# One gather job per block, later blank fills and a later planned landing in a self-scheduled attention and router kernel

## The chip, the cores and the metric

The kernel runs on one core of a Trainium2 chip. The metric is the device time of one execution in microseconds (us). The core has a matrix engine (PE, with its weight loads as PEld), a vector engine (DVE), a scalar engine (ACT), a general engine (POOL) and a queue engine (SP) that mostly starts transfers. Each engine runs its instructions in the order in which the program lists them; the engines wait for each other by semaphores.

## The reference, cut to what matters

```
def phi(x):                                   # 8 x 8 products of two small projections
    a = einsum('rd,bhsd->bhsr', S1, x); b = einsum('rd,bhsd->bhsr', S2, x)
    return einsum('bhsi,bhsj->bhsij', a, b).reshape(..., 64)
q_p, k_p = phi(q), phi(k)                     # q, k, v: 4 batches, 4 heads, 1088 tokens, 32 wide
kv  = einsum('bhsf,bhsd->bhfd', k_p, v);  z = k_p.sum(axis=2)
x   = (q_p @ kv) / (q_p @ z + 1e-6)           # 4352 tokens x 128
noisy = x @ w_gate + log1p(exp(x @ w_noise)) * noise
top2, weights = two best of 8 experts per token, softmax of the two
out[t] = sum over the two experts e of t: weight * (relu(x[t] @ w1[e]) @ w2[e])   # 128 -> 1024 -> 128
```

## The kernel before, in words

**Waves and blocks.** The tokens are routed in five waves: the first half of batch 0 (wave 0, 512 tokens), the rest of batch 0 (wave 1), and batches 1, 2 and 3 (waves 2, 3 and 4). `router` picks the two experts of each token of a wave and their rows, and POOL scatters the scaled tokens (`xg`) by indirect DMAs into the DRAM table `xs`, which has a stretch of rows for every expert ("xs<-xg,to"). Rows that no token may fill are zeroed beforehand by seven blank fills, `clear(0)` to `clear(6)` ("xs<-pad"). A scatter waits for the fills of the rows that its wave can reach: wave 2 for fills 0 to 3, wave 3 for 0 to 4, wave 4 for all.

`block(u, ...)` is one expert's share of a wave: 128 tokens for u below 16, 256 later, 128 again in the last wave of blocks. Its tokens are fetched from `xs` into `xb`, turned into `bT`, multiplied with w1 (`hp`, line 1117), passed through ReLU on ACT (`h`, line 1125), multiplied with w2 (`acc`, line 1132), copied to `y` and scattered by POOL to the DRAM table `pairs`. Blocks 0 to 3 don't go through DRAM: one-hot squares (`o` or `h` tiles) gather their tokens straight from `x` by four matmuls each (line 1074). Blocks 4 to 7 are fetched by POOL's own queue and turned on PE (line 1096). From block 8 on SP fetches (four DMAs a block) and DVE turns (line 1106). The row numbers of a wave come by a small fetch `ix`.

**The attention.** Per batch: DVE turns k and q (`kT`, `qT`, lines 577 and 579), PE projects them (`feat`, line 595), DVE turns the result (`ab`, line 603) and multiplies out `phk` and `phq` (line 618), PE sums `kv` (line 665) and folds the gate weights in (line 686), then turns `phq` (line 713, copied by ACT to `pT`) and multiplies it with the folded table (line 724, copied by ACT to `nd`). From `nd` DVE makes the gates of the router.

**What sets the order.** Nothing is scheduled by hand. Each piece of work is a `Job` with engines, an estimated cost, a landing time (`lat`), a priority and its data. `Plan.order` runs a small model: at each step it takes, of the jobs that could start soonest, the one with the lowest priority number, and so writes one list for every engine. SP transfers take part in a model of the DMA rate, and `lanes` limits how many transfers are planned in flight. PSUM tiles come from pools of two buffers each (`bank`, `feat`, `hp`, `acc`); `bank` serves the gather, the turned blocks, lines 713 and 724 and the counts. Only the order comes from the model; on the chip the waits come from the data. The transfers marked `held`, late inputs and late fills, also wait on the chip for POOL's four fetches.

Of the kernel before, what the change touches and what calls it, by code (L numbers as in the profile page):

```python
# [36 lines left out]
class Plan:  # L37
# [50 lines left out]
    def order(self):  # L88
# [18 lines left out]
        while cand:  # L107
# [37 lines left out]
            if j.size is not None:  # L145
                moved = max(moved, j.end + 0.6) + j.size / self.RATE
                j.done = max(j.done, moved + 0.8 if e == "SP" else j.end + 1.4 + 2 * j.size / self.RATE)
                if e != "POOL":
                    lanes.append(j.done)
            j.opens = [b for b in j.opens if not b.placed]  # L150
            for b in j.opens:
                b.placed = True
# [23 lines left out]
def kernel(  # L176
# [27 lines left out]
    C = 8  # L204
# [30 lines left out]
    def add(engines, cost, emit, **kw):  # L235

        if hold and engines in ("DVE", "PE"):
            kw["after"] = tuple(kw.get("after", ())) + tuple(hold)
        elif hold and engines == EV:
            engines = "ACT"  # L240
        return plan.add(engines, cost, emit, **kw)
# [70 lines left out]
    def mm(n):  # L312
        return max(0.205, 0.016 + 0.00162 * n)
# [477 lines left out]

    BLANK = [(80, 128), (216, 256), (472, 512), (728, 768), (984, 1024), (1024, 1088), (1088, STATIC)]

    def clear(i, prio):
        lo, hi = BLANK[i]

        def done(ins):
            for w in range(NW):
                if REACH[w] <= lo:
                    apart(ins, "scatter%d" % w)  # L800
            wrote(ins, "clear%d" % i)
        g = 16 if (hi - lo) % 16 == 0 else 8
        n = (hi - lo) // g
        dma("SP", lambda: xs_e[:, lo:hi, :].rearrange("e (p c) x -> p e (c x)", c=n),
            lambda: pad[0:g, 0:n * XW].unsqueeze(1).to_broadcast([g, E, n * XW]), ["pad"], [("clear", i)], prio,
            size=4.2e3 * (hi - lo), issue=0.8, done=done, held=i > 2)

    def blanks(w):
        return [i for i, (lo, hi) in enumerate(BLANK) if lo < REACH[w]]
# [11 lines left out]
    def router(b, t0, n, w, x, den, lg, prio):  # L821
# [161 lines left out]
        for t in range(n):  # L983
            rows = slice(0, HB if t0 + t == C else P)
            xg = new("xg")
            pool_job(0.19, prio + 0.8, lambda t=t, xg=xg: G.tensor_copy(
                xg.t[:, :, D:XW].bitcast(I32), pid[:, :, b, t0 + t:t0 + t + 1]), [(xg, 9)], ["pid"])
            if den is None:
                dve(vec(2 * D), lambda t=t, xg=xg: V.tensor_tensor(
                    out=xg.t[:, :, 0:D], in0=x.t[:, t:t + 1, :].to_broadcast([P, 2, D]),  # L990
                    in1=B_["g"].t[:, :, t:t + 1].to_broadcast([P, 2, D]), op=ALU.mult), [x, "g"], [(xg, 0), (xg, 1)], late, [indexed])
            for i in range(2):
                if den is not None:
                    pool_job(gtt(D), prio + 0.9, lambda t=t, i=i, xg=xg: G.tensor_tensor(  # L994
                        out=xg.t[:, i, 0:D].rearrange("p (h d) -> p h d", h=H), in0=x.t[:, t, :, 0:DH],
                        in1=dg.t[:, i, t, :].unsqueeze(2).to_broadcast([P, H, DH]), op=ALU.mult), [(xg, i)], [x, dg], sent[-2:-1])

                def emit(e, t=t, i=i, rows=rows, xg=xg):
                    ins = pool_scatter(den is None, out=xs[:], in_=xg.t[rows, i, :], in_offset=None,
                                       out_offset=bass.IndirectOffsetOnAxis(ap=to.t[rows, i, t:t + 1], axis=0))  # L1000
                    apart(ins, "scatter", "fetch", *("clear%d" % i for i in range(len(BLANK)) if i not in blanks(w)))
                    behind(ins, *("clear%d" % i for i in blanks(w)))
                    wrote(ins, "scatter", "scatter%d" % w)
                sent.append(add("POOL", 1.67 if den is None else 1.2, emit, r=[to, (xg, i), (xg, 9)] + [("clear", i) for i in blanks(w)],
                    w=[("rows", (w, t, i))], prio=prio + 1, lat=LAND + (0.7 if w == 0 else 0.0)))
                routed.setdefault(w, []).append(("rows", (w, t, i)))
        return picked

# [35 lines left out]
    def block(u, w, e, r, n):  # L1044
# [5 lines left out]
        if u < DIRECT:  # L1050
# [7 lines left out]
            def part(c):  # L1058
                return oh.t[:, c, :] if u < DIRECT - 1 else oh.t[:, P * c:P * c + P]
# [10 lines left out]
                    r=["place", onehot["pos"], onehot["gm"]] + ([less] if u == DIRECT - 1 else []), w=[(oh, c)],  # L1070
                    prio=-900 if u == 0 else 12 + u)

            for c in range(4):
                add("PE", mm(P), lambda _, c=c: T.matmul(
                    turn.t[:, 0:P], lhsT=onehot["x"].t[:, c, :], rhs=part(c), start=(c == 0), stop=(c == 3)),
                    lat=0.15, r=[(oh, c), (onehot["x"], c - c % 2)], w=[turn], prio=p0 - 88)
        else:
            xb = new("xb")

# [208 lines left out]
    load_kq(1, "q", 45)  # L1288
    for e in range(2, E):
        load_w(e, 46 + e)  # L1290
    for i in range(2, len(BLANK)):
        clear(i, 60 if i == 2 else 290 + 2 * i)
    x, den, lg, last = queries(0, 0, 4, 10, True)
    picked = router(0, 0, 4, 0, x, den, lg, 12)
    pair_numbers(0, 0, 1, "POOL", 15)
# [6 lines left out]
    for b in range(1, B):  # L1302
        if b > 1:
            load_kq(b, "k", 80 + 100 * b)
            load_kq(b, "q", 81 + 100 * b)
            load_v(b, 82 + 100 * b)
            keys_values(b, 100 * b)
        x, den, lg, last = queries(b, 0, C + 1, 100 * b + 10)
        router(b, 0, C + 1, b + 1, x, den, lg, 100 * b + 20)
        hold.clear()  # L1310
    look(500)
    u = 0
# [64 lines left out]
```

## Time and profile before

| | us |
|---|---|
| median of three runs (lowest, highest) | 351.43 (350.46, 353.52) |
| the profiled execution | 351.54 |
| its span, first to last instruction | 349.8 |
| PE busy in the span | 325.2 |
| POOL busy | 245.4 |
| ACT busy | 137.3 |
| DVE busy | 130.9 |

Busy times of different engines overlap. The profiled execution is 1.7 us longer than its span and within 0.1 us of the median. The mean granted PE clock over the span is 0.975 of full speed.

### The profile page before, as it was taken

The numbers are of one execution on the slowest core, as the hardware profiler recorded it, in microseconds if no ns is written. First come the engines' busy times: TensorE is split into PE (matmuls) and PEld (weight loads), VectorE is DVE, ScalarE is ACT, GpSimd is POOL, SyncE is SP. The second block draws the span as 40 slices with busy tenths as digits, with TensorE's granted clock in tenths as the row PEclk, the third lists the DMA queues.
The fourth block names the chain that finished last, engine by engine and source line by source line (L and its number), as shares of the span: only waits on it lengthen the run. The fifth ranks groups of instructions, "written<-read, shape, count | busy, mean of one in ns | idle before, by whom it ended". The sixth has DMA issues, their size and how long they took to land.

```text
span 349.8 us, 8036 instructions
## 1 busy us (share of the span) xinstructions
PE 325.2 (93%) x2897; PEld 296.0 (85%) x2897; DVE 130.9 (37%) x503; ACT 137.3 (39%) x295; POOL 245.4 (70%) x466
## 2 busy tenths in 40 slices
PE   6889999996999999999999999999999999999940
PEld 2558799795979998999998999999999999999930
DVE  5889698695698719510001110012002000002001
ACT  1336445542544553333432444333433343334310
POOL 7847836968899888888898989979953345354430
PEclk9999999997899999999999999999999999999985
DMA  7999949863311155325223232255334111117103
GB/s 192 272 250 347 359 113 222 140 182 56 71 36 40 39 67 89 75 33 91 59 57 54 55 69 61 53 161 142 66 108 142 31 28 30 32 41 240 51 20 93
DMA packets 66795, 37.31 MB, mean 107 GB/s; under 512 B 48879, under 2 KB 59793, under 8 KB 66752
## 3 DMA queue, kind: packets, MB, share of 16 engines
q1 hardware_dynamic: 61344, 26.87, 33.5%
q0 software_dynamic: 4768, 9.23, 8.2%
q10 hardware_dynamic: 640, 0.67, 0.7%
q8 instruction: 23, 0.38, 0.5%
q14 instruction: 20, 0.16, 0.2%
HBM read 24.17 MB, written 12.83 MB: 106 GB/s over the span
## 4 chain that ended last, share of the span: by engine, by line
PE 40%; issue 20%; POOL 17%; DVE 11%; DMA 6%; ACT 3%; SPq 1%; POOLq 0%; DVEq 0%; ACTq 0%
PE hp L1117 17%; PE acc L1132 17%; POOL pairs L815 9%; POOL pause L816 5%; POOL xs L815 3%; DVE phq L618 2%; DMA kq<-in_q_dram 2%; DMA xs<-xg,to 2%; PE bank L724 2%; ACT h L1125 1%; PE feat L595 1%; PE bank L713 1%; POOL xg L994 1%; DMA pr<-pairs 1%; SPq L332 1%
## 5 line engine op out<-in xcount | busy, mean ns | idle before, releaser
L1132 PEld LDWEIGHTS acc<-w2s,h 128*128 128x128 f32 x1152 | 146.2, 192 | 8.3 <-ACT h L1125 2.4
L1132 PE MATMUL acc<-w2s,h 128*128 128x128 f32 x1152 | 151.0, 276 | 1.6 <-ACT h L1125 1.4
L1117 PE MATMUL hp<-bT,w1s 128*128 128x128 f32 (+1 forms) x768 | 150.1, 332 | 0.0
L1125 ACT ACTIVATE h<-hp 128x512 f32<-128x512 f32 x144 | 85.7, 597 | 125.1 <-PE hp L1117 104.5
L1117 PEld LDWEIGHTS hp<-bT,w1s 128*128 128x128 f32 x768 | 113.8, 195 | 5.8 <-ACT bT L322 0.4
L815 POOL DMA_INDIRECT pairs<-y,mine x72 | 73.4, 1020 | 57.1 <-ACT y L322 45.2
L815 POOL DMA_INDIRECT xs<-xg,to x72 | 74.3, 1032 | 21.1 <-POOL xg L994 8.1
L1106 DVE STREAM_TRANSPOSE bT<-xb 128x256 f32<-128x256 f32 (+1 forms) x40 | 15.6, 389 | 140.7 <-PE hp L1117 104.8
L816 POOL MEMSET pause<- 1x512 bf16 (+1 forms) x144 | 46.8, 325 | 0.1
L994 POOL TENSOR_TENSOR xg<-nd,dg 128x128 f32<-128x128 f32 x64 | 28.4, 445 | 3.3 <-DVE dg L961 3.3
L322 ACT COPY y<-acc 128x128 f32<-128x128 f32 (+1 forms) x48 | 15.3, 318 | 21.7 <-PE acc L1132 14.8
L1164 DVE TENSOR_TENSOR o<-pr 128x512 f32<-128x512 f32 (+2 forms) x12 | 6.8, 567 | 43.3 <-DMA pr<-pairs 41.2
L724 PEld LDWEIGHTS bank<-kvw,pT 128*128 128x128 f32 x128 | 15.2, 192 | 1.7 <-issue 1.4
L724 PE MATMUL bank<-kvw,pT 128*128 128x98 f32 x128 | 16.4, 276 | 0.2 <-ACT pT L322 0.2
L713 PE MATMUL bank<-ident,phq 128*128 128x128 f32 x72 | 12.0, 288 | 3.1 <-DVE phq L618 2.5
L322 ACT COPY pT<-bank 128x512 f32<-128x512 f32 (+1 forms) x20 | 10.8, 544 | 5.8 <-PE bank L713 4.0
L1339 PE MATMUL hp<-zb 128*128 128x512 bf16 x42 | 11.7, 426 | 1.4 <-POOL zb L434 1.4
L618 DVE TENSOR_TENSOR phk<-ab 128x512 f32<-128x512 f32 (+1 forms) x20 | 12.8, 694 | 0.0
L713 PEld LDWEIGHTS bank<-ident,phq 128*128 128x128 f32 x72 | 8.2, 147 | 5.3 <-ACT vaug L637 2.5
L618 DVE TENSOR_TENSOR phq<-ab 128x512 f32<-128x512 f32 (+1 forms) x20 | 12.5, 659 | 0.1
L322 ACT COPY nd<-bank 128x392 f32<-128x392 f32 (+1 forms) x18 | 7.9, 449 | 8.9 <-PE bank L724 6.5
L603 DVE STREAM_TRANSPOSE ab<-feat 64x32 f32<-64x32 f32 (+2 forms) x32 | 7.6, 283 | 9.0 <-PE feat L595 6.0
(166 smaller groups left out, 196.2 us busy)
## 6 DMA issues: line engine op xcount, KB each, us to landing
w1s<-in_moe_w_dram SPq DMA_DIRECT2D x8, 512.0 KB
w2s<-in_moe_w_dram SPq DMA_DIRECT2D x8, 512.0 KB
xb<-xs SPq DMA_DIRECT2D x96, 32.0 KB
pr<-pairs SPq DMA_DIRECT2D x6, 512.0 KB
kq<-in_k_dram SPq DMA_DIRECT2D x4, 544.0 KB
kq<-in_q_dram SPq DMA_DIRECT2D x4, 544.0 KB
vld<-in_v_dram SPq DMA_DIRECT2D x14, 128.0 KB
out_dram<-o SPq DMA_DIRECT2D x6, 256.0 KB
```

The lines of the kernel that those rows point to most:

```text
L322: A.copy(o, i) if e == "ACT" else V.tensor_copy(o, i)
L618: (V if e == "DVE" else G).tensor_tensor(out=dst.t[rows, c0 + i:c0 + m, :, :].rearrange("p c h (i j) -> p (c h) i j", i=R), in0=f[:, :, 0, ...
L713: T.transpose(ps.t[:, c0:c0 + P], pq.t[:, t + i, 2 * a:2 * a + 2, :].rearrange("p h f -> p (h f)"), ident[:])
L724: T.matmul(ps2.t[:, c0:c0 + 2 * YW], lhsT=pT.t[:, P * (2 * i + a):P * (2 * i + a) + P], rhs=kvw.t[:, a, :], start=True, stop=True)
L815: ins = G.indirect_dma_start(**kw)
L816: G.memset(pause[:, 0:PAUSE if fill else 2], 0.0)
L994: pool_job(gtt(D), prio + 0.9, lambda t=t, i=i, xg=xg: G.tensor_tensor(out=xg.t[:, i, 0:D].rearrange("p (h d) -> p h d", h=H), in0=x.t[:, ...
L1106: add("DVE", vec(P * n), lambda _: V.transpose(bT.t[:, 0:P * n], flat()), r=[xb], w=[bT], prio=TOP + u)
L1117: T.matmul(hp.t[:, P * n * i:P * n * (i + 1)], lhsT=w1s[:, e, P * (js * g + i):P * (js * g + i + 1)], rhs=bT.t[:, 0:P * n], start=True, st ...
L1125: A.activation(out=h.t[:], in_=hp.t[:], func=AF.Relu)
L1132: T.matmul(acc.t[:, D * c:D * c + D], lhsT=h.t[:, P * (n * i + c):P * (n * i + c + 1)], rhs=w2s[:, e, j, :], start=(j == 0 and c == 0), st ...
L1339: T.matmul(began[0][:], lhsT=zb[:, 0:P], rhs=zb[:], start=True, stop=True)
```

## The change: what it does

Three edits of the planner's input. The four gathering matmuls of block 0 stay four jobs, since the first squares come one by one; those of blocks 1 to 3 become one job of four matmuls each. Blank fills 4, 5 and 6 get a later priority and may be planned only after the mask of wave 1's router, and a late fill's planned issue time grows from 0.8 to 1.7 us. The planned landing of wave 1's scatters grows by 1.5 us, and `lanes` now counts a transfer by its own issue and the DMA rate, without the job's landing time. No instruction is added or removed; the planner writes another order.

```diff
-                    lanes.append(j.done)
+                    lanes.append(max(j.end + 2.3, moved + 0.8 if e == "SP" else 0.0))
...
-    def clear(i, prio):
+    def clear(i, prio, after=()):
...
-            size=4.2e3 * (hi - lo), issue=0.8, done=done, held=i > 2)
+            size=4.2e3 * (hi - lo), issue=1.7 if i > 2 else 0.8, done=done, held=i > 2, after=after)
...
-                    w=[("rows", (w, t, i))], prio=prio + 1, lat=LAND + (0.7 if w == 0 else 0.0)))
+                    w=[("rows", (w, t, i))], prio=prio + 1, lat=LAND + (0.7, 1.5, 0.0, 0.0, 0.0)[w]))
...
-            for c in range(4):
-                add("PE", mm(P), lambda _, c=c: T.matmul(
-                    turn.t[:, 0:P], lhsT=onehot["x"].t[:, c, :], rhs=part(c), start=(c == 0), stop=(c == 3)),
-                    lat=0.15, r=[(oh, c), (onehot["x"], c - c % 2)], w=[turn], prio=p0 - 88)
+            def gathered(_, cs):
+                for c in cs:
+                    T.matmul(turn.t[:, 0:P], lhsT=onehot["x"].t[:, c, :], rhs=part(c), start=(c == 0), stop=(c == 3))
+            for cs in ((0,), (1,), (2,), (3,)) if u == 0 else (range(4),):
+                add("PE", mm(P) * len(cs), lambda _, cs=cs: gathered(_, cs), lat=0.15,
+                    r=[(oh, c) for c in cs] + [(onehot["x"], c - c % 2) for c in cs], w=[turn], prio=p0 - 88)
...
-    for i in range(2, len(BLANK)):
-        clear(i, 60 if i == 2 else 290 + 2 * i)
+    clear(2, 60)
+    clear(3, 296)
...
-        router(b, 0, C + 1, b + 1, x, den, lg, 100 * b + 20)
+        picked = router(b, 0, C + 1, b + 1, x, den, lg, 100 * b + 20)
+        if b == 1:
+            for i in range(4, len(BLANK)):
+                clear(i, 390 + 2 * i, (picked,))
```

On PE, after block 0's second product, block 2's gather came in two halves, and block 3's as one matmul and, behind batch 1's k projection, three. Now block 1's and block 3's come whole and at once, block 1's `hp` and eight matmuls of line 713 follow, and then block 2's gather, whole too. Three places show what else has moved.

On DVE, from the turned k projection of batch 1 (`ab`) on, before: all of `phk` and the q projection come first, then wave 1's gates (`den`).

```order
L603 STREAM_TRANSPOSE ab<-feat 128x8x32
L603 STREAM_TRANSPOSE ab<-feat 64x32
L618 TENSOR_TENSOR phk<-ab 128x512 x4
L618 TENSOR_TENSOR phk<-ab 64x256
...
L618 TENSOR_TENSOR phq<-ab 128x512
L735 TENSOR_SCALAR den<-nd 128x20
```

After, wave 1's router is worked in between; its row numbers (`to`) now come before most of `phk` and all of `phq`.

```order
L603 STREAM_TRANSPOSE ab<-feat 128x8x32
L603 STREAM_TRANSPOSE ab<-feat 64x32
L735 TENSOR_SCALAR den<-nd 128x20
...
L618 TENSOR_TENSOR phk<-ab 128x512
L870 TENSOR_SCALAR up<-u 128x40
...
L618 TENSOR_TENSOR phk<-ab 128x512 x2
L922 TENSOR_SCALAR g<-g 128x5
...
L955 CAST to<-at 128x2x5
```

The factors `dg` stood ahead of `to` before and stand behind it now.

On SP, from batch 2's inputs to wave 1's fetches, before:

```order
L332 DMA vld<-in_v_dram 32x4x32 x2
L332 DMA xs<-pad 8x8x645 x2
L332 DMA xs<-pad 16x8x516 x2
L332 DMA kq<-in_k_dram 128x1088
L332 DMA kq<-in_q_dram 128x1088
...
L332 DMA ix<-xs 128x8x1
L332 DMA xb<-xs 32x4x32 x32
L332 DMA ix<-xs 128x8x1 x2
```

After:

```order
L332 DMA vld<-in_v_dram 32x4x32 x2
L332 DMA xs<-pad 8x8x645
L332 DMA kq<-in_k_dram 128x1088
L332 DMA kq<-in_q_dram 128x1088
...
L332 DMA xb<-xs 32x4x32 x32
L332 DMA xs<-pad 8x8x645
L332 DMA xs<-pad 16x8x516 x2
L332 DMA ix<-xs 128x8x1 x2
```

Fills 4, 5 and 6 have moved from between the inputs of batches 2 and 3 to behind wave 1's 32 fetches, ahead of wave 2's.

On PE, at the first block of wave 1 (block 8): before, everything of block 7, batch 2's sum (665) and the wave's counts (913, 916) stood ahead of the queries (713).

```order
L1132 MATMUL acc<-w2s,h 128x128 x8
L665 MATMUL bank<-phk,vaug 33x64 x36
L913 LDWEIGHTS earlier
...
L713 MATMUL bank<-ident,phq 128x128 x4
L686 MATMUL feat<-wg_71,kvT 64x49 x4
L1117 MATMUL hp<-bT,w1s 128x128 x12
```

After:

```order
L1134 MATMUL acc<-w2s,h 128x128 x8
L665 MATMUL bank<-phk,vaug 33x64 x36
L1119 MATMUL hp<-bT,w1s 128x128 x12
L1134 MATMUL acc<-w2s,h 128x128 x8
L686 MATMUL feat<-wg_71,kvT 64x49 x4
L1119 MATMUL hp<-bT,w1s 128x128 x4
```

Of the twelve `hp` matmuls the last four are block 8's, which need its `bT`; block 7's second product and the counts stand behind them.

## Rows read from the trace of the kernel before

**Rows 1.** Windows of 1 us, PE alone: length, busy (instructions), clock, DMA share, GB/s.

```profile
80.00:81.00 1.00, 0.86 (x23) 1.00 0.76 62
81.00:82.00 1.00, 0.19 (x2) 1.00 0.30 61
82.00:83.00 1.00, 0.00 (x0) 1.00 0.43 99
83.00:84.00 1.00, 0.02 (x1) 0.62 0.27 39
84.00:85.00 1.00, 1.00 (x4) 0.50 0.24 36
```

**Rows 2.** Timeline of PE there: start, us, operation, [idle before <- releaser].

```profile
78.19 2.33 PE L665 MATMUL bank<-phk,vaug 128*33 128x64 f32 x72
83.98 1.09 PE L713 MATMUL bank<-ident,phq 128*128 128x128 f32 x4 [2.46 <-DVE phq L618]
```

**Rows 3.** Timeline of DVE at the wait.

```profile
82.86 0.31 DVE L1106 STREAM_TRANSPOSE bT<-xb 128x128 f32<-128x128 f32 x1 [3.68 <-DMA xb<-xs]
```

**Rows 4.** The chain that ended last, wave 1's last scatter: start, us, what.

```profile
72.59 5.81 DMA xs<-xg,to
```

**Rows 5.** Timeline of SP: how long it took to issue fills, inputs, fetches.

```profile
55.73 6.80 SPq L332 DMA_DIRECT2D xs<-pad  x4
68.51 3.41 SPq L332 DMA_DIRECT2D vld<-in_v_dram  x6
78.63 0.39 SPq L332 DMA_DIRECT2D ix<-xs  x1
79.07 16.84 SPq L332 DMA_DIRECT2D xb<-xs  x32
124.14 1.12 SPq L332 DMA_DIRECT2D ix<-xs  x2
```

**Rows 6.** Windows of 2 us: PE, PEld, DVE, ACT, POOL, clock, DMA share, GB/s.

```profile
64.00:66.00 2.00, 1.85 (x39) 1.02 (x37) 1.92 (x7) 0.82 (x3) 1.80 (x4) 1.00 0.87 114
70.00:72.00 2.00, 2.00 (x20) 2.00 (x19) 1.93 (x5) 0.66 (x3) 1.83 (x4) 1.00 1.03 366
```

**Rows 7.** Timeline of DVE at wave 1's router.

```profile
45.51 0.18 DVE L735 TENSOR_SCALAR den<-nd 128x20 f32<-128x20 f32 x1 [0.19 <-ACT nd L322]
53.48 1.50 DVE L618 TENSOR_TENSOR phq<-ab 128x512 f32<-128x512 f32 x2
56.13 0.17 DVE L955 CAST to<-at 128x10 uint32<-128x10 f32 x1
```

**Rows 8.** The chain that ended last: pieces of PE's work, each matmul as two.

```profile
97.35 1.10 PE feat L595 x24
...
99.97 0.92 PE acc L1132 x8
```

**Rows 9.** Timeline of POOL: scaling and scatters of waves 1 and 2.

```profile
53.72 1.52 POOL L994 TENSOR_TENSOR xg<-nd,dg 128x128 f32<-128x128 f32 x2 [3.31 <-DVE dg L961]
57.10 1.32 POOL L815 DMA_INDIRECT xs<-xg,to  x1 [1.86 <-issue]
120.68 0.95 POOL L815 DMA_INDIRECT xs<-xg,to  x1 [0.21 <-issue]
```

**Rows 10.** Timeline of ACT: one copy of line 713's result to `pT`.

```profile
49.32 0.58 ACT L322 COPY pT<-bank 128x512 f32<-128x512 f32 x1
```

**Rows 11.** Windows of 1 and 5 us, PE alone, with the old order's small waits.

```profile
96.00:97.00 1.00, 0.86 (x9) 1.00 0.40 33
...
110.00:115.00 5.00, 4.78 (x48) 1.00 0.12 40
...
120.00:125.00 5.00, 4.67 (x41) 1.00 0.13 30
```

**Rows 12.** Timeline: wave 2's first turned block on DVE, its first use on PE.

```profile
129.56 0.45 DVE L1106 STREAM_TRANSPOSE bT<-xb 128x256 f32<-128x256 f32 x1 [8.71 <-DMA xb<-xs]
134.75 1.03 PE L1117 MATMUL hp<-bT,w1s 128*128 128x256 f32 x4
```

## The prediction

> **What bounds the kernel now.** The first view is the page's busy table: PE works 325.2 of 349.8 us, so only what makes PE stand still, or run slowly, can be won. Its slices over the span show three soft places: the start, a hole a little past 80 us, and the tail after PE's last product. The change touches neither end, so the hole is the one to read. In windows of 1 us [rows 1] PE is busy 0.86, 0.19, 0.00 and 0.02 us between 80 and 84: 1.07 of 4, so **2.93 us idle**. While it stood, the granted clock fell to 0.50, that is from 2.4 to 1.2 GHz, and it stayed there until 90 (five more windows like the last one shown). Six us of work at half speed are three us of work at full speed, so the clock cost **3.0 us** more. Together the hole costs 5.9 us, 1.7% of the run. What clock comes back to PE is worth as much as what idle time does.
>
> Why does PE stand? It waits for DVE's `phq` [rows 2], but DVE was not busy: it had sat 3.68 us in front of a `bT` that waits for wave 1's first fetched block, and `phq` stands behind that in DVE's order [rows 3]. The fetch was late because wave 1's last scatter, issued at 72.59, landed 5.81 us later [rows 4]; SP started `ix` at 78.63 [rows 5], and the first `bT` began at 82.86, 4.23 us after. So the chain is: wave 1's router on DVE, ten scatters on POOL, landing, fetch, DVE, PE.
>
> **The change, part by part.** The profiled execution took 351.54 us, within 0.1 of the median, so sums are made against it. No instruction comes or goes; the gathers, the fills and the scatters cost what they cost. What counts is the order.
>
> *Router earlier.* On PE, one group of `acc` matmuls, two groups of `hp` and batch 1's q projection now come behind the last of batch 0's queries instead of ahead of it: 0.9 + 2 x 0.9 + 1.1 = 3.8 us, a group of `hp` taken as one of `acc` [rows 8]. Against it stands a new wait, below, of 0.5. So batch 0's `nd` is complete, and DVE starts wave 1's gates, 3.3 us earlier: at 42.2 instead of 45.51 [rows 7], since DVE now does little in front of it. From there to the end of `to` DVE took 45.51 to 56.30, 10.8 us, with four pieces of `phq` in between; now three pieces of `phk` of the same shape (0.75 each by the `phq` row [rows 7], which is the dearer end) and two turns of `ab` lie there, so I take 11.0, and `to` ends at 53.2. The counts on PE are then done: by the same count of groups PE reaches them near 51. But `dg` now stands behind `to`, so POOL's two scalings of 1.52 us, which before were over when `to` came [rows 9], now follow it: 53.2 + 0.2 + 1.5, then 0.2 to 0.8 of hand-over (before, 0.8 passed between `to` and the scatter). The first scatter starts at 55.1 to 55.7 instead of 57.10, **1.4 to 2.0 us earlier**, and the last, 15.5 us behind the first as before, at 70.6 to 71.2.
>
> *Landing.* Fills 3 to 6 took SP 6.80 us to issue [rows 5], and between 64 and 66 us the DMA engines were 87% busy at only 114 GB/s [rows 6]. Behind that came the inputs of batch 3; when the last scatter of wave 1 was sent, they moved 366 GB/s at full share [rows 6], the last of them issued from 68.51 on for 3.41 us [rows 5]. Three of the four fills now lie elsewhere: 3 x 1.7 = 5.1 us less on SP. Of that some is lost, because k and q of batch 3 wait for DVE's turns of batch 2's, now later, and v for ACT's copies; I reckon that v of batch 3 goes out 3 to 4 us earlier and is in by about 70. Then the last scatter lands like wave 2's, sent at 120.68 with `ix` at 124.14, 3.46 us after [rows 5, 9], not 5.81. I take 3.46, because the loads that ran beside the slow one are through; 5.81 stays as the other end. SP's `ix` goes at 74.0 to 74.7, and the first `bT` of wave 1, 4.23 later, is done at 78.6 to 79.2; with a landing of 5.81 it is 81.0 to 81.6.
>
> The Trainium skill bears on this step (DMA: Bandwidth & Descriptors, Queues, rings and completion order): each DMA engine takes the queues that have work in turn, a packet at a time. By that rule SP's fills and loads hold up a scatter on POOL's queue by their share alone, and no run here shows the engines' turns. The sum would then go by the loaded end, the first rival's.
>
> *Does PE still wait there?* PE finished batch 2's sum (line 665) at 80.5 [rows 2]. In the new order the same work, less block 7's second product (two groups, 1.8), stands ahead of block 8's first `hp`, so PE would come there at 78.7 with no new wait. The rows also give the new waits. Block 2's gather needs a `bank` buffer that ACT frees by a `pT` copy (0.58 [rows 10]) behind two ReLUs: 0.5 to 0.6. Batch 1's q projection needs a `feat` buffer that DVE frees only after the gates: 0.3. Block 4's turn may stand 0 to 0.5 in front of its fetch. In batch 1's queries groups of lines 713 and 724 now hand the two `bank` buffers to each other with little else between: 0.1 to 0.3 four times. That is 1.0 to 2.4; a wait of 0.15 that the old order has between 64 and 66 goes [rows 6]. Net **0.8 to 2.2, taken 1.4**, so PE comes at 79.5 to 80.9, after the `bT`. Then nothing empties, the clock holds, and the whole 5.9 comes back less the new waits.
>
> *Later.* The same hand-over of `bank` comes in batch 2 (two waits of 0.25) and, with nothing between at all, in batch 3 (four of 0.2 to 0.3, since a `pT` copy with its semaphores is longer than the 713 group that should cover it [rows 10]): 1.1 to 1.6, less the 0.14, 0.22 and 0.33 that the old order idles there [rows 11]: **0.4 to 0.9, taken 0.5**. The price of a hand-over is an estimate, worked out from that copy alone.
>
> *Fills 4 to 6* stand on SP behind wave 1's 32 fetches, which ended at 95.9 [rows 5]. Behind them wait wave 2's `ix` and fetches, not due before 124 [rows 5], and wave 3's scatters on POOL, which come after wave 2's last at 120.68 [rows 9]. Some 25 us of cover; if it failed, they would cost their 5.1 us of issue. I set 0. *Wave 2* had its first `bT` at 130.0 and PE used it at 134.75 [rows 12]: 4.7 us to spare, more than the gain, and its scatters start earlier too.
>
> *Sum:* 5.9 - 1.4 - 0.5 = 4.0 us, **347.5 us**; by the ends 5.9 - 0.8 - 0.4 = 4.7 and 5.9 - 2.2 - 0.9 = 2.8, so 346.8 to 348.7.
>
> **The rivals.** *The landing stays slow and the clock falls again.* `bT` is done at 81.3, PE stands 0.5 to 2 us in front of block 8, though block 7's second product and the counts (2.2 us) stand ready behind it. Where PE stood at 83.98 before, it would be at 83.6: 0.4 won, the 3.0 of clock lost again, 0.5 lost later: 351.6. For it: other loads still run near 70 us. Against it: PE stood 2.9 us before the clock fell, and here less; without the fall it is 348.6, inside the forecast's range.
>
> *Hand-overs eat the gain.* If each of some 14 hand-overs of `bank` waits 0.35 (a `pT` copy and its semaphores against a 713 group), that is 4.9, and less the 0.8 of old waits 4.1: 5.9 - 4.1 = 1.8, 349.7, from 348.7 to 350.5. For it: two buffers and one copying engine. Against it: ACT is busy 137.3 of 349.8 us only.
>
> *Slower.* The price of block 8's `hp` ahead of ready work: with `bT` done at T, PE is 2.2 us later where it stood at 83.98 before. With the clock falling again and 0.5 later, the change breaks even at T = 81.2; at the old 83.2 it gives 353.5; from T = 84.7 it is over 1% slower, 355.1. That takes scatters 1.5 us later than before, say from a router held by `nd`.
>
> **How the numbers follow.** 1% (3.5 us) is about what a measurement of this kernel tells from no change. The forecast (346.8 to 348.7, 347.5) gets 0.52, hand-overs 0.22, slow landing with the clock 0.15 (350.5 to 352.5), slower 0.11. The range is 345.6 to 351.6: the low end 1.2 under the forecast's, in case other work hides the new waits, the high end to the middle of the slow landing; outside lie 0.11 and some 0.08. Faster by over 1% means below 347.9, some three quarters of the forecast, with what lies under it 0.42; slower by over 1%, 0.10; the rest 0.48.
>
> **What the new profile would show.** Right: the first scatter of wave 1 near 55.4, its last landing in under 4 us, the first `bT` of wave 1 before 79.5, no window with the clock at 0.50 between 75 and 100, and PE's idle time spread in waits of 0.2 to 0.6 on ACT's copies. Wrong: a hole over 1 us in front of block 8 or a fallen clock (the first rival), or idle time of over 4 us in small pieces from 31 to 130 (the second). The forecast fails altogether if PE finds another hole, in front of batch 2's or 3's `phq` say, since the whole order after 31 us is new.

## The result, and the profile after

| | before | after |
|---|---|---|
| median of the comparison (lowest, highest), us | 350.89 (348.38, 353.52) | 347.89 (346.31, 354.72) |
| the profiled execution, its span, us | 351.54, 349.8 | 346.66, 344.8 |
| mean granted PE clock over the span | 0.975 | 0.985 |

The ratio is **0.9916, interval 0.9890 to 0.9942**: 3.0 us, 0.8%, faster. The forecast was 347.5. (The highest time after, 354.72, belongs to a slow execution that the ratio leaves out.) The two profiled executions lie 4.9 us apart, more than the medians, since the changed kernel's is one of its quick ones. One correction to the text on the change: fills 4 to 6 wait for the mask of wave 2's router, that of batch 1, not of wave 1's.

The hole is gone. Windows of 1 us of the changed kernel, PE alone, which answer to [rows 1]:

```profile
81.00:82.00 1.00, 1.00 (x12) 1.00 0.38 83
82.00:83.00 1.00, 1.00 (x15) 1.00 0.33 54
83.00:84.00 1.00, 1.00 (x11) 1.00 0.47 94
```

PE is busy throughout and the clock stays at 1.00, that is 2.4 GHz. PE's timeline of the changed kernel there, beside [rows 2]:

```profile
75.43 2.33 PE L665 MATMUL bank<-phk,vaug 128*33 128x64 f32 x72
77.69 3.00 PE L1119 MATMUL hp<-bT,w1s 128*128 128x128 f32 x24
80.53 1.95 PE L1134 MATMUL acc<-w2s,h 128*128 128x128 f32 x16
...
84.94 0.63 PE L713 MATMUL bank<-ident,phq 128*128 128x128 f32 x4
```

Each matmul of the order shows as two here. The last eight of the 24 `hp` matmuls are block 8's, and no bracket of a wait stands there. The chain in front of them, on POOL (beside [rows 9]; the bracket is the idle time ahead):

```profile
53.14 0.77 POOL L994 TENSOR_TENSOR xg<-nd,dg 128x128 f32<-128x128 f32 x2 [2.42 <-DVE stops L966]
54.06 1.08 POOL L815 DMA_INDIRECT xs<-xg,to  x1 [0.16 <-POOL xg L994]
...
69.77 0.92 POOL L815 DMA_INDIRECT xs<-xg,to  x1 [0.21 <-POOL pause L816]
...
99.59 0.19 POOL L986 COPY xg<-pid 128x2 int32<-128x2 int32 x1 [1.65 <-DMA xs<-xg,to]
```

The first scatter of wave 1 starts at 54.06 (57.10 before), the last at 69.77 (72.59). SP's timeline, beside [rows 5]:

```profile
66.00 3.41 SPq L332 DMA_DIRECT2D vld<-in_v_dram  x6
72.16 0.39 SPq L332 DMA_DIRECT2D ix<-xs  x1
72.60 18.62 SPq L332 DMA_DIRECT2D xb<-xs  x32
91.26 3.27 SPq L332 DMA_DIRECT2D xs<-pad  x3
122.35 1.03 SPq L332 DMA_DIRECT2D ix<-xs  x2
```

The `ix` fetch, which waits for the last scatter, follows it by 2.39 us, not 6.04 (72.59 to 78.63). On DVE, beside [rows 3] and [rows 7], the gates, the row numbers and the first turned block:

```profile
41.31 0.55 DVE L735 TENSOR_SCALAR den<-nd 128x20 f32<-128x20 f32 x1 [0.35 <-ACT nd L322]
...
52.71 0.17 DVE L955 CAST to<-at 128x10 uint32<-128x10 f32 x1
...
78.13 0.31 DVE L1108 STREAM_TRANSPOSE bT<-xb 128x128 f32<-128x128 f32 x1
```

That `bT` waits for nothing any more. So far all is as forecast, or better. What was not forecast is the last line of POOL's timeline above: beside the moved fills, POOL stands 1.65 us in the middle of wave 2's scatters. Where that leads, e11 and e12 show.

### The profile page after: what moved, and what is told of

Read it like the earlier page. It is cut to its first block, busy times and chain, and to the rows that moved or that the text cites. A ratio compares the mean times of both kernels' runs of the same rounds, so it can differ in the third digit from the quotient of the medians.

```text
span 344.8 us, 8044 instructions
## 1 busy us (share of the span) xinstructions
PE 323.3 (94%) x2894; PEld 293.7 (85%) x2897; DVE 132.6 (38%) x503; ACT 137.2 (40%) x295; POOL 243.3 (71%) x466
## 4 chain that ended last, share of the span: by engine, by line
PE 33%; POOL 27%; issue 14%; DMA 14%; DVE 7%; ACT 2%; SPq 1%; POOLq 1%; DVEq 0%; ACTq 0%
POOL pairs L815 14%; PE acc L1134 14%; PE hp L1119 13%; DMA pairs<-y,mine 8%; POOL pause L816 7%; POOL xs L815 4%; DMA xs<-xg,to 2%; PE bank L724 2%; DMA kq<-in_q_dram 2%; POOL xg L994 2%; PE feat L595 1%; PE bank L665 1%; SPq L332 1%; DMA pr<-pairs 1%; ACT h L1127 1%
## 5 line engine op out<-in xcount | busy, mean ns | idle before, releaser
L1119 PE MATMUL hp<-bT,w1s 128*128 128x128 f32 (+1 forms) x768 | 148.1, 328 | 0.0
L1119 PEld LDWEIGHTS hp<-bT,w1s 128*128 128x128 f32 x768 | 111.5, 191 | 5.5 <-ACT bT L322 0.4
L815 POOL DMA_INDIRECT pairs<-y,mine x72 | 72.1, 1002 | 56.5 <-ACT y L322 47.4
L994 POOL TENSOR_TENSOR xg<-nd,dg 128x128 f32<-128x128 f32 x64 | 27.5, 432 | 2.4 <-DVE stops L966 2.4
L618 DVE TENSOR_TENSOR phq<-ab 128x512 f32<-128x512 f32 (+1 forms) x20 | 13.9, 736 | 0.1
L1344 PEld LDWEIGHTS <-zb 128*128 128x128 bf16 x42 | 4.3, 109 | 6.6 <-issue 2.2
```

What stands on the lines that cost most here:

```text
L618: (V if e == "DVE" else G).tensor_tensor(out=dst.t[rows, c0 + i:c0 + m, :, :].rearrange("p c h (i j) -> p (c h) i j", i=R), in0=f[:, :, 0, ...
L815: ins = G.indirect_dma_start(**kw)
L1119: T.matmul(hp.t[:, P * n * i:P * n * (i + 1)], lhsT=w1s[:, e, P * (js * g + i):P * (js * g + i + 1)], rhs=bT.t[:, 0:P * n], start=True, st ...
L1344: T.matmul(began[0][:], lhsT=zb[:, 0:P], rhs=zb[:], start=True, stop=True)
```

## The experiments

They ran on four chips, called A (e1 to e4), B (e5 to e8), C (e9, e10) and D (e11, e12); which chip the comparison above ran on is not on record. Ratios are always against the kernel before on the same chip.

**e1: the changed kernel with fills 4 to 6 back in their old place** (chip A); only SP's list differs.

```diff
-    clear(2, 60)
-    clear(3, 296)
+    for i in range(2, len(BLANK)):
+        clear(i, 60 if i == 2 else 290 + 2 * i)
```

> The changed kernel with one thing undone: fills 4 to 6 are planned as before, so they stand on SP next to fill 3 again, ahead of batch 3's inputs. The order of PE, DVE, ACT and POOL is word for word that of the changed kernel; only SP's differs. My theory (the fills and what they push back make wave 1's last scatter land late): the first scatter at 54 as in the changed kernel, the last at 69.8, but a landing of 5 to 5.8 us instead of 2.39, so SP's row numbers go at 75 to 75.6 and block 8's first turned block is there at 79.5 to 81.5. PE comes for it at 79.5, so it stands 0 to 2 us there; without a fall of the clock 348 to 350, with one 351 to 352. Rival (the earlier router alone sets the landing; the fills are beside the point): a landing of 2.4 to 3.5 and 347.9, no change against the changed kernel.

Measured: 353.54 against 352.01, ratio 1.0040 (1.0010 to 1.0070), slower than either side expected. PE's timeline of e1, and then ACT's:

```profile
77.84 2.05 PE L1119 MATMUL hp<-bT,w1s 128*128 128x128 f32 x16
83.10 1.31 PE L1119 MATMUL hp<-bT,w1s 128*128 128x128 f32 x8 [3.21 <-issue]
84.21 3.46 PE L1134 MATMUL acc<-w2s,h 128*128 128x128 f32 x16
```

```profile
75.69 0.27 ACT L322 COPY y<-acc 128x128 f32<-128x128 f32 x1 [0.69 <-issue]
80.89 0.26 ACT L322 COPY kvT<-bank 33x128 f32<-33x128 f32 x1 [4.93 <-PE hp L1119]
...
82.45 0.60 ACT L1127 ACTIVATE h<-hp 128x512 f32<-128x512 f32 x1 [1.19 <-remote]
```

PE stands 3.21 us in front of block 8, and the next 16 matmuls take 3.46 instead of 1.95 us, at half the clock. It looked as if the fills' place were the whole change. But ACT's copy of line 665's sum comes 5.3 us after that sum began (75.58), where the changed kernel's comes 2.37 us after (75.43 to 77.80), and behind the copy stands the ReLU (82.45 to 83.05) that frees one of the two `hp` buffers, at whose end PE goes on. DVE had turned block 8's first tokens by 81.11. So of the 3.21 us the late landing accounts for 1.2 (PE was free at 79.89) and ACT's lateness for the other 2.0. Two delays were mixed here; in e11 the second is absent.

**e2: the changed kernel without the gather edit** (chip A).

```diff
-            for cs in ((0,), (1,), (2,), (3,)) if u == 0 else (range(4),):
+            for c in range(4):
```

> The changed kernel with the other thing undone: the gathers of blocks 1 to 3 are four jobs of one matmul again. Wave 1's gates go back behind batch 1's phk and first phq on DVE, the fills stay late. My theory counts two gains that add up, 1.4 to 3 us from the earlier router and 2.3 to 3.4 from the landing: here only the landing is left, the first scatter at 57, the last at 72.6, row numbers at 75 to 76, first turned block at 79 to 80.5. PE's own order is another one as well (batch 1's queries later), so the hole closes if PE comes after 80 and the time is 347.5 to 349.5. Rival (the early router is what closes the hole): a hole of 1 to 3 us and a fallen clock somewhere between 75 and 90, 350 to 352.

Measured: 348.38, ratio 0.9904 (0.9873 to 0.9936), as expected. `ix` goes at 74.19, 2.0 us later than in the changed kernel, yet on this chip the kernel gains as much as the whole change did in its own comparison.

**e3: the kernel before with the hole filled**, eleven matmuls on zeros ahead of batch 2's first 713 group (chip A). They compute nothing that is used.

```diff
+                if b == 2 and t == 0:
+                    for _ in range(11):
+                        T.matmul(ps.t[:, 0:512], lhsT=zb[:, 0:P], rhs=zb[:], start=True, stop=True)
```

> The kernel before with 11 idle products of 128x512 zeros on PE (bf16, as at the start of the kernel), put ahead of batch 2's first matmuls of line 713, that is into the hole between 80.5 and 84; they write a bank tile that the next matmuls overwrite, so the result doesn't change. The wait itself stays. My theory (of the hole's 5.9 us 3.0 are the clock): no interval of the clock at 0.50 between 80 and 91, PE still without useful work for 2.9 us, and 3.0 us less: 347.9 against 350.9. Rival (the fall of the clock is not caused by the hole, or costs little): 350.5 to 351.5.

Measured: 351.75, ratio 0.9990 (0.9961 to 1.0019), not the 3.0 us less that I expected. Windows of 2 us of e3, PE alone, where the kernel before had the clock at 0.50:

```profile
84.00:86.00 2.00, 2.00 (x19) 1.00 0.21 29
86.00:88.00 2.00, 2.00 (x19) 1.00 0.29 57
```

The clock holds. From the 713 group to the next `acc` group PE takes 5.11 us (84.78 to 89.89) where it took 7.83 before (83.98 to 91.81): 2.72 less, nearly the 3.0 that the prediction put on the clock. Of that, some 1.3 went to fillers that ran on past the end of the wait (the first `phq` was done at 83.3). Most of the rest is given back 30 us later; PE's timeline of e3:

```profile
119.59 0.66 PE L716 MATMUL bank<-ident,phq 128*128 128x128 f32 x4 [1.53 <-ACT nd L322]
```

ACT's copy to `nd` had waited 1.60 us for POOL, whose scatters of wave 2 still read one of the two `nd` buffers. PE's wait there is 0.20 in the first profile of the kernel before, which came 0.7 us later. So the clock's price was right, and POOL's train of scatters is the next bound.

**e4: the changed kernel with the copies to `pT` and `nd` planned 0.2 us longer** (chip A), so that the planner itself spaces the hand-overs of `bank`.

```diff
-r=[ps], w=[pT], prio=prio)
+r=[ps], w=[pT], prio=prio, lat=0.2)
...
-r=[ps2], w=[(nd, t - t0)], prio=prio)
+r=[ps2], w=[(nd, t - t0)], prio=prio, lat=0.2)
```

> The changed kernel with two numbers of the planner raised: the copies to pT and to nd of batches 1 to 3 count 0.2 us more until their result is free. The planner then puts other matmuls between the groups of lines 713 and 724 that hand the two bank buffers to each other (PE's order in batch 3 goes from 713, 724, 713, 724, 713, 724, 713, 724 in a row to groups with w1 or w2 products between them). My theory (these hand-overs cost 0.9 us in batch 1 and 1.0 in batches 2 and 3): 1 to 2 us less than the changed kernel, 346 to 347, if block 8's first turned block still comes in time. Rival (PE only waits elsewhere, for instance on wave 1's first fetches, which PE now reaches sooner): no change or up to 1 us more, 347.5 to 349.

Measured: 355.88, ratio 1.0117 (1.0075 to 1.0158), worse than either side expected. Batch 2's 72 narrow matmuls of line 665 came in bits there, from 70.81 on, with gaps of up to 0.47 us that the profile puts down to no wait. Gaps of 0.2 to 0.3 stand in such a sum in other profiles from A and B too (e2, e3, e5 to e8) and in none from C and D, so whether the new order or the chip broke it up is not shown. Windows of e4, PE alone:

```profile
76.00:80.00 4.00, 3.86 (x44) 0.50 0.36 74
80.00:84.00 4.00, 4.00 (x25) 0.50 0.33 63
```

Eight us and more at half clock hide whatever the hand-overs gave. The price of a hand-over can't be read from this kernel.

**e5: the kernel before with the fills' edit alone** (chip B).

```diff
-    for i in range(2, len(BLANK)):
-        clear(i, 60 if i == 2 else 290 + 2 * i)
+    clear(2, 60)
+    clear(3, 296)
...
+        if b == 1:
+            for i in range(4, len(BLANK)):
+                clear(i, 390 + 2 * i, (picked,))
```

> The kernel before with the late fills alone: fills 4 to 6 get their later priority, their later earliest time and the issue estimate of 1.7 us; gathers, planned landing and lanes stay as they were. My theory by now (the landing of wave 1's last scatter behind SP's queue is the cause of the hole, the earlier router only adds to what is there already): the last scatter near 72, a landing near 2.4, row numbers near 74.2 and no hole over 1 us in front of block 8: 347.5 to 349, a ratio to the kernel before of 0.988 to 0.993. Rival (the planned landing of wave 1's scatters is needed as well, since the plan now puts block 8's first turned block ahead of wave 2's row numbers on DVE): DVE stands 0.5 to 2 us in front of that turned block and PE after it, 349.5 to 351.

Measured: 347.74 against 351.83, ratio 0.9899 (0.9854 to 0.9944). The last scatter goes at 72.81 and `ix` at 75.19, 2.38 us later.

**e6: the changed kernel with the planned landing as before**, that is without both edits of the planned times (chip B).

```diff
-                    lanes.append(max(j.end + 2.3, moved + 0.8 if e == "SP" else 0.0))
+                    lanes.append(j.done)
...
-lat=LAND + (0.7, 1.5, 0.0, 0.0, 0.0)[w]))
+lat=LAND + (0.7 if w == 0 else 0.0)))
```

> The changed kernel without its two edits of the planned times: the landing of wave 1's scatters counts 2.2 us again instead of 3.7, and the lanes count a transfer to its planned end. The early router and the late fills stay. On SP the last two, small pieces of batch 3's v now stand behind wave 1's 32 fetches instead of ahead of them, and DVE turns two blocks ahead of wave 2's factors. My theory (these two edits move nothing that is late): the changed kernel's time, 347.5 to 348.5, ratio 0.989 to 0.994. Rival (batch 3's v comes some 20 us later and its copies stand on ACT ahead of ReLUs): a hole of 1 to 4 us on PE between 95 and 112, 349 to 353.

Measured: 353.20, ratio 1.0056 (1.0026 to 1.0086). `ix` goes at 71.68, the earliest so far, and block 8's first tokens are turned by 79.41. But ACT's copy of line 665's sum again comes late (75.58 to 81.47), PE stands 2.08 us for a ReLU behind it, until 82.91, and the clock falls. That is about the rival's time, but its hole was expected elsewhere, between 95 and 112. The late copy hides what the edit is worth.

**e7 and e8: three `nd` buffers instead of two**, in the changed kernel and in e2's (chip B), paid for with fewer `y` buffers.

```diff
-    tag("nd", 2, [P, C + 1, H, YW])
+    tag("nd", 3, [P, C + 1, H, YW])
...
-    tag("y1", 13, [P, D])
-    tag("y2", 10, [P, 2 * D])
+    tag("y1", 8, [P, D])
+    tag("y2", 6, [P, 2 * D])
```

> The changed kernel with three nd buffers instead of two; to make room the result buffers y1 and y2 go from 13 and 10 to 8 and 6, which changes the order only far behind, in the last blocks. In the changed kernel ACT's copy to nd at 118.80 waits 0.84 us for POOL, which still reads that nd buffer for wave 2's scatters, and PE waits 0.67 and 0.36 us around it. My theory (POOL's scatters hold the buffer, and that is where some of the later gain stays): ACT's copy no longer waits for POOL, PE's two waits at 118 to 123 shrink to under 0.3 together, and PE reaches block 8's followers 0.6 to 0.9 us earlier: 347.0 to 347.4. Rival (those waits are the hand-over of the two bank buffers alone): they stay at 0.3 to 0.4 each, 347.8 to 348.2.

> The kernel with gathers in four pieces, late fills and both planned times (the run that measured 0.9904), and with three nd buffers, y1 and y2 at 8 and 6. If nd buffers held by POOL are what stops PE later, this version, whose wave 2 goes out 8 us earlier than the changed kernel's, has little to gain from the third buffer: 347.5 to 348.5. If the third buffer frees the order of batch 3 in both versions, 346.5 to 347.5, the best of all. Against both: fewer y buffers make PE wait for POOL's scatters of pairs late in the run, which would show as waits of acc or ACT on POOL behind 150 us, 348.5 to 350.

Measured: 362.32 (1.0310, 1.0261 to 1.0359) and 392.80 (1.1168, 1.1121 to 1.1215). One line of e8's list of PE's waits (total, times, longest):

```profile
PE acc L1132 <- ACT y L322: 42.5, 1, 42.5
```

PE stood 42.5 us once for a `y` buffer (in e7 3.7 us once, and 3.3 us once for a ReLU). Both miss every time expected, and that swamps the question; whether a third `nd` buffer pays stays open.

**e9 and e10: the two kernels unaltered, on one chip** (C).

> The changed kernel itself, unaltered, on another chip and with another profile. In its first profile batch 2's sum (line 665) was answered by ACT's kvT copy 2.37 us after its start, in every other profile, the kernel before's too, 3.7 to 7.7 us after it. If that belongs to the kernel (my theory of the hole is then complete as it stands): again 2.4 us, a span near 345 and 347.5 to 348.5. If it belongs to the one execution (rival: PE runs late behind these sums in most executions of either kernel, and the first profile was a lucky one): 3.5 to 5 us, idle time of 1 to 2 us on PE near 80, and a time of 348 to 350 for the profiled execution. The median over rounds should be 347.5 to 348.5 either way.

> The kernel before itself, unaltered. Its ratio to itself shows how far these comparisons can be trusted: 0.997 to 1.003. If the hole between 80 and 84 belongs to the kernel: DVE again stands over 3 us in front of block 8's first turned block, the last scatter of wave 1 again lands 5 to 6 us after its issue, and the clock falls once between 80 and 95. If it was that one execution's: a landing under 4 us in this profile.

Measured: e9 348.09 against 350.23, ratio 0.9941 (0.9906 to 0.9977); e10 350.25, 0.9993 (0.9964 to 1.0023). This pair of profiles gives the cleanest account, though e9's is the quickest of its twelve executions (345.80), so that the two lie further apart than the medians' 2.1 us. It is read at points where both have done the same work: e10 had done by 73.69 what e9 had done when it began batch 2's sum at 74.84 (1.15 behind); at the `hp` behind batch 2's queries it is 4.96 ahead (123.58, 128.54); at PE's end 5.02 ahead (330.11, 335.13). So 6.1 us are won between 75 and 124, and nothing is lost behind. PE's timeline of e10:

```profile
84.62 0.89 PE L713 MATMUL bank<-ident,phq 128*128 128x128 f32 x4 [4.51 <-DVE phq L618]
...
120.36 0.66 PE L713 MATMUL bank<-ident,phq 128*128 128x128 f32 x4 [1.59 <-ACT nd L322]
...
128.54 2.90 PE L1117 MATMUL hp<-bT,w1s 128*128 128x128 f32 x24
```

And of e9, at the work of that last line:

```profile
123.58 2.93 PE L1119 MATMUL hp<-bT,w1s 128*128 128x128 f32 x24
```

The hole in e10 is 4.51 us. The granted clock fell with the end of it (0.92, 0.50 three times, 0.87 from 84 to 89): 0.08 + 1.50 + 0.13 = 1.7 us more. In e9 there is none of it; its own waits for `nd` at that second place are 0.67 and 0.36, against 1.59. That makes 4.51 + 1.7 + 0.6 = 6.8 for the 6.1; small waits take the rest.

**e11 and e12: e1's kernel once more, and the change, on one chip** (D).

> The kernel of the first experiment again (the changed kernel with fills 4 to 6 back ahead of batch 3's inputs; all other engines' orders are those of the changed kernel), now on the same chip as the changed kernel itself. The two chips on which the first eight experiments ran gave profiles in which PE's results of line 665 are signalled 1.3 to 5.4 us late, and the changed kernel was not among them; so the 353.5 measured there may hold two causes. My theory (the fills alone): a landing of 5 us or more, PE standing 1.5 us or more in front of block 8, and 3 to 5 us more than the changed kernel on this chip, whatever the signals do. Rival (PE's late signals made it slow, the fills little): within 1 us of the changed kernel here.

> The changed kernel once more, as the partner of the run above. If this chip's profile shows line 665 answered within 2.4 us everywhere, as the chip of the last two runs: 347.5 to 348.5 and a ratio to the kernel before of 0.990 to 0.995. If it shows late answers of 3.5 to 6 us in batches 2 and 3, as on the first two chips: PE waits 1 to 3 us behind batch 2's sum, since ACT's copy of that sum stands ahead of the ReLUs that free the two hp buffers, and the time is 351 to 353.5, no better than the kernel before there (351.8 to 352.0). The latter would mean that the kernel without planned landing and lanes, measured at 353.2 there, lost nothing by that.

Measured: e11 347.53 against 349.78, ratio **0.9931** (0.9905 to 0.9957); e12 348.62, ratio **0.9955** (0.9923 to 0.9986), its median just above the 348.5 expected. The two intervals overlap. With the fills in their old place the kernel is no slower here, against 1.0040 on chip A: the rival of e11, not my 3 to 5 us more. In e11 ACT's copy of line 665's sum comes 2.38 us after the sum began (75.28, 77.66), so the other delay of e1 is absent, and what the fills do stands alone. POOL's timeline of e11:

```profile
69.62 0.91 POOL L815 DMA_INDIRECT xs<-xg,to  x1 [0.21 <-POOL pause L816]
...
90.60 0.97 POOL L815 DMA_INDIRECT xs<-xg,to  x1 [1.72 <-issue]
```

Windows of 2 us of e11, all engines, then clock, DMA share and GB/s:

```profile
70.00:72.00 2.00, 2.00 (x20) 2.00 (x20) 1.65 (x4) 0.48 (x2) 0.98 (x5) 1.00 0.91 334
72.00:74.00 2.00, 2.00 (x21) 2.00 (x20) 1.86 (x6) 1.10 (x3) 1.43 (x3) 1.00 1.11 208
...
94.00:96.00 2.00, 2.00 (x19) 1.78 (x17) 1.49 (x5) 0.86 (x2) 1.84 (x5) 1.00 0.32 68
```

The same windows of the changed kernel:

```profile
70.00:72.00 2.00, 2.00 (x21) 2.00 (x20) 1.50 (x4) 0.47 (x2) 1.84 (x6) 1.00 0.25 58
...
94.00:96.00 2.00, 2.00 (x41) 1.35 (x40) 0.70 (x3) 0.55 (x2) 1.83 (x6) 1.00 0.87 125
```

With the fills early, SP's inputs of batch 3 still run when the last scatter goes: DMA share 0.91 and 1.11, and `ix` follows at 76.37, 6.75 us after. PE's timeline of e11 shows what that costs:

```profile
81.28 1.13 PE L1119 MATMUL hp<-bT,w1s 128*128 128x128 f32 x8 [1.69 <-DVE bT L1108]
...
84.92 0.44 PE L686 MATMUL feat<-wg,kvT 33*64 33x49 f32 x8 [0.73 <-DVE ab L603]
```

That is 2.42 us, and the clock holds. With the fills late, the share is 0.25 and the scatter lands in 2.39 us, but the fills now load the engines 20 us later, beside wave 2's scatters: 0.87 instead of 0.32. POOL, which began that train of scatters 2.3 us earlier than e11 (88.27, 90.60), stands 1.65 us in it for an `xg` buffer whose scatter has not landed, and ends it only 0.7 earlier (last scatter 120.18, 120.90). What follows from that is read on DVE, in the changed kernel and then in e11:

```profile
127.43 0.45 DVE L1108 STREAM_TRANSPOSE bT<-xb 128x256 f32<-128x256 f32 x1 [8.92 <-DMA xb<-xs]
```

```profile
128.23 0.45 DVE L1108 STREAM_TRANSPOSE bT<-xb 128x256 f32<-128x256 f32 x1 [7.52 <-DMA xb<-xs]
```

The first `bT` of wave 2 comes only 0.8 us earlier. Wave 3's router stands behind it on DVE; ACT's exponential of that router (`u`) stands ahead of two ReLUs. ACT's timeline and then PE's of the changed kernel:

```profile
131.61 0.26 ACT L852 ACTIVATE u<-u 128x72 f32<-128x72 f32 x1 [2.42 <-DVE u L850]
```

```profile
124.17 2.93 PE L1119 MATMUL hp<-bT,w1s 128*128 128x128 f32 x24
...
132.71 1.16 PE L1134 MATMUL acc<-w2s,h 128*128 128x128 f32 x8 [1.17 <-ACT h L1127]
138.64 1.16 PE L1134 MATMUL acc<-w2s,h 128*128 128x128 f32 x8 [0.39 <-ACT h L1127]
139.63 0.60 PE L1119 MATMUL hp<-bT,w1s 128*128 128x256 f32 x2
```

PE's timeline of e11 at the same work:

```profile
126.19 2.93 PE L1119 MATMUL hp<-bT,w1s 128*128 128x128 f32 x24
...
139.70 0.60 PE L1119 MATMUL hp<-bT,w1s 128*128 128x256 f32 x2
```

At 124 the changed kernel is 2.02 us ahead, at 139.6 it is 0.07 ahead. The late fills save 2 us at block 8, and PE then waits for wave 2 instead, whose train they held up; e11, coming later, has no wait there. In e9, on another chip, only the first of the two waits is there, and 1.3 of 2.6 us are left (123.58 against 126.19, 138.38 against 139.70), so how much is given back differs by execution.

In e12, the changed kernel itself, this went furthest. POOL's timeline, then ACT's and PE's of e12:

```profile
101.85 0.20 POOL L986 COPY xg<-pid 128x2 int32<-128x2 int32 x1 [3.77 <-DMA xs<-xg,to]
```

```profile
120.99 0.48 ACT L322 COPY nd<-bank 128x392 f32<-128x392 f32 x1 [2.87 <-POOL xg L994]
```

```profile
121.53 1.13 PE L724 MATMUL bank<-kvw,pT 128*128 128x98 f32 x8 [2.69 <-ACT nd L322]
```

Windows of 1 us of e12, PE alone:

```profile
122.00:123.00 1.00, 1.00 (x10) 0.94 0.15 33
123.00:124.00 1.00, 0.95 (x5) 0.50 0.12 29
...
129.00:130.00 1.00, 1.00 (x7) 0.65 0.51 66
```

POOL waits 3.77 us for its buffer, so its train ends late; the last scaled tokens hold an `nd` buffer; ACT's copy waits for that, PE for the copy, and then the clock falls for seven windows (0.06 + 6 x 0.50 + 0.35 = 3.4 us). In the changed kernel's first profile the same chain costs PE 0.67 at 119.34, and the clock holds. POOL's break is 1.65 us there and 1.87 in e9, and 3.23, 2.22 and 4.61 in e6, e4 and e7; none of the profiles with the fills early (before, e1, e3, e10, e11) has one. When the train starts does not decide it: with the fills late it broke though it began only at 91.5 to 96.3 (e4, e6, e7), with the fills early it began at 90.0 to 93.3 and did not. With the fills late but the gather in pieces it is 0.79 (e5) or none (e2, whose train began at 81.97, ten us ahead of its fills).

The single times fit this. Of the changed kernel's 43 executions in the comparison, e9 and e12 (all but the 354.72), 32 had a mean clock of 0.978 or more and took 345.8 to 348.8 us; eleven had 0.970 to 0.976 and took 349.1 to 351.5. e12's profile (0.976, 349.70) is one of the eleven. e11's twelve executions all had 0.980 or more and took 346.5 to 349.2. That all eleven fell at the same place was not looked at, since only one of them was profiled.

## Why the prediction was right, and the step of it that failed

**The total** was 347.5, that is 4.0 us less than the profiled 351.54. The medians give 3.0 us, inside the forecast's 2.8 to 4.7 but near its low end; 351.54 lies 0.65 above the median before, so part of the closeness to 347.89 is luck.

**The hole** was priced at 5.9 us, 2.93 idle and 3.0 of clock. Both parts hold: the hole closed, the clock stayed up, and e3 got 2.72 us of clock by itself. The size differs by execution (4.51 + 1.7 in e10).

**Router earlier** was right and undersized: 3.0 us at the first scatter (in the pair on chip C 56.84 to 53.47, 3.4) where 1.4 to 2.0 were forecast. The gates began at 41.31, not 42.2; `to` came at 52.71, not 53.2; and the two scalings behind `dg` took 0.77 us, not the 1.52 of [rows 9], with 0.16 of hand-over.

**Landing** was put at 3.46 us; it is 2.39 in the changed kernel, and 2.3 to 2.4 in each one with the fills late but e7 (3.2). With the fills early it is 6.0 (before), 5.8 (e3), 6.1 (e10), 6.75 (e11) and 7.4 (e1), all from the last scatter to `ix`. The low end is not where I took it, because I read it from a scatter of wave 2, and it is lower than both rows that I bounded it with. The Trainium skill (DMA: Bandwidth & Descriptors, Queues, rings and completion order) has each DMA engine take the queues with work in turn; that a loaded queue of SP's holds up a scatter of POOL's agrees with it in direction, by 3.4 to 5.0 us.

**The new waits up to 75 us** came to 1.2 net (1.24 in the pair on chip C) where 1.4 were taken. They sit on 713 groups (0.9) and batch 1's q projection (0.6), with 0.3 got back on `acc`; the one named first, block 2's gather for `pT`, waits 0.29 instead of 0.5 to 0.6. The hand-over rival asked for 4.1 us and is out. The sums were not right, though: the items add up to 1.2 to 2.6, not 1.0 to 2.4, and those of *Later* to 1.3 to 1.7, not 1.1 to 1.6, which would have made the forecast 347.3 to 349.1.

**The step that failed** is the cover of the fills, and with it that of wave 2: "Some 25 us of cover; if it failed, they would cost their 5.1 us of issue. I set 0", and "4.7 us to spare, more than the gain, and its scatters start earlier too". The cover was counted in deadlines: what stands behind the fills on SP, and which scatters need those rows. Neither was late. What the fills met is traffic that doesn't depend on them, wave 2's scatters, which were under way at that time in the kernel before already (from 90.55, in the run of [rows 9]). They now start 2.3 us earlier but end only 0.5 earlier (120.18, 120.68). And the 4.7 us to spare were read at PE's first use of the `bT`, not at the router that stands behind it on DVE, which PE meets sooner by way of ACT. Where the clock holds, this costs PE 0.67 at 119 and 1.17 to 1.56 at 131 to 139 (e9, first profile); in e12 2.69 and 3.4 of clock. The sum came out all the same because the kernel before can wait at the same places for the same reasons: 1.59 and 1.10 in e10, though only 0.20 and 0.76 in its first profile.

**Later waits** were to cost 0.5 net. The brackets between 85 and 124 are 0.19, 0.67 and 0.36 in the changed kernel's first profile and in e9, against 0.22 and 0.20 in the first profile of the kernel before, 0.8 less, and 1.59 in e10, 0.4 more. So the net was 0.8 in one pair and -0.4 in the other. Behind 124 nothing is lost: in the pair on chip C the lead is 4.96 us at 124 and 5.02 at the end.

**The first rival** named the other case correctly: a slow landing without a fall of clock, "348.6, inside the forecast's range". e11 is that case, at 347.5. Its reason against a fall, that PE stood 2.9 us before the clock fell, misreads [rows 1]: the window from 83 to 84 has 0.62 while PE is still idle, so the clock fell after some 2.2 us (an estimate from these windows). It held through 1.69 us in e11 and fell after 2.08 in e6. So the prediction's total was right, but the part of it that it gave to the landing is no part of the gain measured on chip D: the 2 us that the late fills save at block 8 are given back at wave 2, all of them in the first profile and half in e9, and in e12 more than that is lost. What is left for the gain there is the order with the earlier router, from the gather edit and the planned landing together; no run parts those two on such a chip.

**Open.** On chips A and B the same question came out the other way: the fills' edit alone gave 0.9899 (e5), and the change without it 1.0040 (e1). My conclusion from these, that the fills are everything, fell with e11. The fills' place does not sort the runs on A and B either: e1 and e6 differ in it, and both lost, with the whole gathers' order and a ReLU for block 8 behind ACT's late copy; e2 and e5 have the gather in pieces, and both gained. So the late copy is the likelier cause there, but that was not tested. None of the experiments timed the changed kernel on A or B, nor e2 and e5 on C or D, so which version is best on a given chip is not known. The planner's landing edits (e6), the price of a hand-over (e4) and a third `nd` buffer (e7, e8) stay open as well.

## What to carry to other kernels

A moved transfer needs two kinds of cover: that nothing behind it is due, and that nothing else on the DMA engines is in a hurry where it lands; look at the DMA share of the stretch it moves to, and at who frees a buffer by a landing there. When a wait is closed, look for the next engine that holds a buffer across the same stretch: here it was POOL's train of scatters, which took about 1.5 us back from e3 and up to 2 from the fills' edit. And time both sides on the same chip before an edit is given the credit: one kernel came out at 1.0040 on one chip and 0.9931 on another.

## What the runs showed of the hardware

One thing I had not expected, and can't explain. On chips A and B, and in the first profile of the kernel before, ACT's copy of line 665's sum for batch 2 starts late after its 72 narrow matmuls. In the kernel before:

```profile
82.25 0.53 ACT L322 COPY kvT<-bank 33x128 f32<-33x128 f32 x2 [3.70 <-PE bank L916]
```

PE had begun that sum at 78.19 [rows 2], so the copy came 4.06 us after; in e10, the same kernel on chip C, 2.38 us after (77.42 to 79.80). In e1 it is 5.3 and in e6 5.9 us; for batch 1 it is 2.4 to 2.8 in every profile. The kernels with a ReLU for block 8 behind the copy fell into the half clock there in e1 and e6, where it was late, and not in the first profile after, e9, e11 and e12, where it was prompt; in e7 it was late (4.5 us) and the clock held behind a stand of 1.55. The kernel before took 352.0 and 351.8 us (medians) on A and B, and 350.2 and 349.8 on C and D, which goes the same way; that the late copies make this difference was not shown.
